# A gated mix of an S4 convolution and a top-2 SwiGLU: identity matrices by GpSimd, one sum of products on TensorE, the last tile pair in two banks, a new order

## The chip, the cores and the metric

The kernel runs on one core of a Trainium2 chip. The time is device microseconds of one execution, as a median of several runs; a profile is taken of one more execution. TensorE (PE) multiplies matrices and writes to PSUM banks; VectorE (DVE), ScalarE (ACT) and GpSimd (POOL) work elementwise; SyncE (SP) and ScalarE issue the DMA transfers of this kernel. Each engine works through its own queue of instructions, and semaphores order them between engines.

## The reference, cut to what matters

```python
x = A_u                                            # 1 x 2048 x 512, bfloat16
g = sigmoid((x * gate_w).sum(-1, keepdims=True))
a = A_ref(x, A_re, A_im, B_re, B_im, C_re, C_im, log_dt, Dskip)
b = B_ref(x, w_r, w_gate, w_up, w_down)
return g * a + (1 - g) * b

# A_ref: S4 convolution, D = 512 channels, N = 128 states, L = 2048
dt = exp(log_dt)[:, None]
P  = exp((dt * A)[:, :, None] * l[None, None, :])  # A, B, C complex
K  = einsum("dn,dnl,dn->dl", C, P, dt * B).real
y  = irfft(rfft(u, 4096) * rfft(K, 4096))[:L] + u * Dskip

# B_ref: the 2 tokens of largest x @ w_r go through silu(x_s @ w_gate) * (x_s @ w_up) @ w_down,
# times sigmoid(r), and are added to x
```

## The kernel before, in words

The convolution is done in the frequency domain with matrix products. Channels are split in two halves h of 256 (HC), tokens in two blocks `blk` of 1024, frequencies in two halves `qd`. The program is a list of some 640 operations, made by these functions in the order of L1133 to L1159:

- *Start* (L558 to L640). Six parameter tables are loaded (PRM 0 to 5: A_re, A_im, C_re, C_im, B_re, B_im), with log_dt and the identity matrix CB, a 64 KB transfer from the constant `c_bf` on SyncE's queue. DTP is exp(log_dt) on ScalarE (L586). DG (L587) is the identity with its columns scaled by DTP, a product on VectorE; RV (L588) is the identity with its columns reversed, a copy on VectorE. PE scales and transposes the parameters with DG (L597) and with the identity (L608); VectorE reduces the phase of A_im to a turn (L625 to L627, seen in the profile as L460, L459, L462) and multiplies B by C (L632, L633).
- `exps1`, `exps2`, `tab1`, `tab2` build tables of powers of exp(dt A). `turns` (L687) adds quarter turns with the identity or its negative (L709), ScalarE takes sines (L720). `trig` (L671) takes a sine, adds 16384 to its angles (L683), and takes another. `tab2` multiplies tables (L745) and joins further ones by two lists; an entry of `MUL2` with n = 1 is two products of 512 elements and a difference and a sum (L751 to L754).
- `routing` transposes u on PE (L802), copies the transposes out of PSUM (L805, four at a time 1024 wide), computes gate and router sums, and runs the two chosen tokens through the feed-forward part.
- `forward` is the transform of u (PE L945, evicted L949). `kgen` sums the kernel K in pieces (PE L964, evicted L968) and `kspec` transforms it (PE L1016, seeded by ScalarE L1009 or PE L1007, evicted L1020) into KK.
- `products(h, qds, blks)` multiplies the spectra on VectorE: p (L1039) and, for block 1, t (L1042), each 4096 wide. For block 1 the two are added (L1059), then a difference and a sum of 1024 give the real and the imaginary part (L1060, L1061), and four operations of 1024 write X (L1066). For (h, qd) = (1, 0) the additions are done by PE instead: L1052 sums p and t in PSUM with the identity and its negative, eight matmuls of 512 for each of the two parts, and L1056 evicts. This is the list `ACC`.
- `inverse(h)` is the transform back, for blocks 1 and 0 and four pairs of token tiles each. PSUM is seeded by ScalarE with u times a gate quotient (L1082), or, for the last pairs, u is scaled in place (L1080); PE adds the frequencies (L1104, eight matmuls per pair and half), and the result is scaled out: by ScalarE for most pairs (L1114), by VectorE's fused multiply-add for the pairs scaled in place (L1123), and for the last pair, tiles 5 and 7 of (h, blk) = (1, 0), in two ScalarE operations (L1126). Then it is stored, two tiles of 128 x 256 in one transfer of 128 KB (L1130).

`TT`, `TS`, `STT`, `CP`, `AC`, `EV`, `SCL` and `DMA` (L454 to L477) are the helpers that record an operation; the profile shows their lines, L455 for every `TT`, for instance. In the profile "L455 DVE TENSOR_TENSOR 128x4096" is therefore any product of that width.

The order is written out by hand. `ORDER` (L371) is a string with the list's indices in the order of work, three characters each; each engine takes its own operations in that order (L132), and `emit` (L160) puts the waits for their inputs in front. `SECOND` says for each operation that can run on two engines, (ACT, DVE) or (DVE, ACT), whether the second is taken; `PLACES` says which PSUM bank or buffer each temporary has. The new order in the change is a new `ORDER`, `SECOND` and `PLACES`.

Of the kernel before, what the change touches and what calls it, by code (L numbers as in the profile page):

```python
# [14 lines left out]
ACTF = mybir.ActivationFunctionType  # L15
ALU = mybir.AluOpType
# [236 lines left out]
ACC = ((1, 0),)  # L253
DIAG = ()
# [102 lines left out]
def small_mats():  # L357
# [15 lines left out]
    "00200r01e01h01i00000101k01m00300500400v00w00700y02000600k00f01000x01400e00800z00b01501w01602101101900900a0b101201z01301a01o01s01b00l01g02l02d01700g01u"  # L373
    "02n0b302e01r02j00h01j02301c02f02h01f02m02p02k03100d01t02g0b400q01d02r02i02o01v00j02u02q02s02t03201y01l03302v02605w02400n09k0b202w01x02a03403502503603g"
    "05v05j03h02702802909j03705k03i05x02x03803j03903k0b502204k00i00m03l00s02y03a03m05q04j00c03n04000p05p03d05e0b603o05d01805r03x03p02z03q03r00t01n03004l0b7"
    "05f06r06p03s06q06s01p03t0b804a03u04m03v0bi04n0bh04103y05l06t04o05y05t04p00u03z03w06u04q05s04204s0bj04r06v05n05m04t06x05u04u0bk04v06w04506z05z03e07006y"
    "0bm0600bl04604z0710760470750bo04304w01q07205g07707804x04c07307a07904805h0bn04906707c06804y07b05005107405i04d0bc05307d07e07o05o05407g0ba04b05204407f04e"
    "04f02c06906e04g07h02b04h05507p05606d0b905706k05806f06n0bb06m05906j0bd07j06g07m06h07r05a08v06o06l07l09l06i06207k05b07q05c0be06107n09m06307s06409n0650bf"
    "07i07t08006a07z07u09o07x09s06606b07y07v0bg08107w0c009p08209t08308408808909q06c0bp09r04i09u08609v08y08508a08c08b0bq08708x09z08i08e08d09w03b08w0br0a00a3"
    "08f0a10a208h0bs08g0by08k08l0bu09x0a60bv09y08j08m0c108n0a70a408p0bw0c20bt0a500o08r0a808u0bx08q0c90bz08o0c30a90aa09b0990ab08z08s0c509c0ac09d09e09a08t0aw"  # L380
    "0910c409f0c60c80ca09g09h0cb0cc09209i0cf0ce0da0900c70ch0ax0al0ay0az0ci0cg0cl0b00ck0960cj0970cd0co0cn0cq0cr0cm0cx0cp0cs0980ak0ct0cu0cv0cw0930cy0cz0db094"
    "03f0d10d00d30d20ev0950d40am0ao0an0d90dn0aq0df0do0ep0dc0ap0d50du0dg0ar0eq0d60dv0dw0dd0ae0dp03c0dh0as0de0di0dk0dq0dj0dl0at0dm0fd0h00dr0ds0eu0dt0d80av0fi"
    "0au0ey0f30ff0fe0eo0f40en0er0fj0d70e10fg0ex0f10fh0fk0ad0e40ew0es0af0gw0f00f70et0f20fl0ah0e50dz0ag0fm0ez0aj0e00fn0e60fo0ai0f50g60fp0gb0fq0e80ed0ea0ga0f6"
    "0f80e20g70ge0gc0eh0dy0gd0fa0gg0fr0g80fs0f90gi0e30fu0ee0ft0dx0fw0fc0e90h40ef0fb0e70eb0ei0eg0gf0g90gj0go0gh0h10ec0gk0gq0gp0gm0fv0fx0h60gx0em0el0h20fy0h7"
    "0gz0gl0gn0h30ej0h50h80ek0h90fz0g00g20hi0g10ha0g30hm0g40gy0hj0gt0g50gr0hk0hl0hn0ho0hb0hc0hp0gs0gv0gu0hs0ht0hd0he0hf0hg0hq0hh0hr"
)
SECOND = (
    "000000000000000000000000000000000000000000000100000000000000000000000000000000000000001010100000101000000000000000000000000000000000000000000000000000"
    "000000000000000000010000001000000100000000000000000000000000000000000000000000000000000000001000100000001000000000000000000000000000000000000000000000"
    "000000000000000000000000000100000000000010000000000000000000000000000000000000000000000000000000011000100000001000000000000000000000000000000000000000"  # L390
    "000000000000000000000000000000000001000000000100100000000000000000000000000000000000000000000000000000000000000000000000000000000000000000000000000000"
    "000000000010000000000000000000000000000000"
)
PLACES = (
    "023476015031122254636201420476642046744011102462062440662046000044406046674020026662010100000000014262646223660464004367063320204022041525736"
# [4 lines left out]
def bass_gated_mix__ssm_conv_s4__moe_arch_mod__prompt_kernel(nc, A_u, A_A_re, A_A_im, A_B_re, A_B_im, A_C_re, A_C_im, A_log_dt, A_Dskip,  # L400
# [24 lines left out]
    with ExitStack() as es:  # L425
# [109 lines left out]
        DD = B("dd", oR + 24 * KB, 4 * KB)  # L535
# [22 lines left out]
        DQ([(CB(0, 128, 0, (1, EK0)), cb_c[:, 0:EK0])], [], [(CB, "i")], 65536)  # L558
# [14 lines left out]
        DQ([(CB(0, 128, EK0, (1, CBW - EK0)), cb_c[:, EK0:])], [], [(CB, "o")], 196608)  # L573
# [14 lines left out]
        CP(RV(0, 128, 0, (1, 128)), CB(0, 128, 127, (-1, 128)), [CBI], [RV])  # L588
# [98 lines left out]
        def turns(h, ts):  # L687
# [23 lines left out]
            for k, g in enumerate((0, 3, 2, 1)):  # L711
# [5 lines left out]
                for x in ("cs" if k % 2 else "sc"):  # L717
                    if x == "sc"[1 - k % 2]:
                        P.op(PE, lambda hh, k=k: quarter(hh, k % 2), [TIB, CBI], [pb], cost=0.4314)
                    AC(so(2 if x == "c" else neg), lo, ACTF.Sin, [pb], [(s, x)], scale=SC16, tset=ts)  # L720
# [17 lines left out]
        def tab2(h, ts):  # L738
# [7 lines left out]
            for o, a, da, b, n in MUL2:  # L746
                A, Bc, O = lambda t: t(0, 128, a * HC, (da * HC, n), (1, HC)), lambda t: t(0, 128, b * HC, (0, n), (1, HC)), lambda t: t(0, 128, o * HC, (HC, n), (1, HC))
                p = lambda i: qa(0, 128, i * n * HC, (HC, n), (1, HC))
                kr = lambda t: [(t, k) for k in ([("e", a + i * da) for i in range(n)] + [("e", b)] if t is eb else [a + i * da for i in range(n)] + [b])]
                ko = lambda t: [(t, ("e", o + i) if t is eb else o + i) for i in range(n)]  # L750
                TT(pair(p(0), p(1)), pair(Bc(eb), Bc(di)), pair(A(eb), A(eb)), MUL, kr(eb) + kr(di), [(qa, 0), (qa, 1)])  # L751
                TT(pair(p(2), p(3)), pair(Bc(di), Bc(eb)), pair(A(di), A(di)), MUL, kr(eb) + kr(di), [(qa, 2), (qa, 3)])
                TT(O(eb), p(0), p(2), SUB, [(qa, 0), (qa, 2)], ko(eb))
                TT(O(di), p(1), p(3), ADD, [(qa, 1), (qa, 3)], ko(di))  # L754
# [40 lines left out]
        def routing():  # L795
# [42 lines left out]
            if DIAG:  # L838
                CP(SGB(0, 128, 64, (1, 16)), SG(0, 128, 96, (1, 16)), [(SG, "x")], [(SGB, "x")])
                TS(SG(0, 128, 0, (1, 16)), SGB(0, 128, 64, (1, 16)), 1.0e-30, ADD, [(SGB, "x")], [(SG, "d")])  # L840
                P.op(DVE, lambda h: h.reciprocal(SG(0, 128, 80, (1, 16)), SG(0, 128, 0, (1, 16))), [(SG, "d")], [(SG, "q")], cost=0.3)
                STT(SG(0, 128, 112, (1, 16)), SG(0, 128, 96, (1, 16)), 1.0e-30, SG(0, 128, 80, (1, 16)), ADD, MUL, [(SG, "x"), (SG, "q")], [(SG, "s")])
                TT(SG(0, 128, 112, (1, 16)), SG(0, 128, 112, (1, 16)), SG(0, 128, 64, (1, 16)), MUL, [(SG, "m")], [(SG, "s")])
# [77 lines left out]
        def late():  # L921
            P.op(POOL, lambda h: h.memset(OHR(0, 128, 0, (1, len(ERT) * 128)), 0.0), [], [OHR], cost=0.4)
            for k in (2, 3, 0, 1) if DIAG else ():
                def dd(h, k=k, act=False):
                    r = None
                    for tb in range(4 * k, 4 * k + 4):
                        o, i, c = DD(0, 128, tb * 128, (1, 128)), CB(0, 128, 0, (1, 128)), SG(0, 128, tb, (1, 1))
                        r = h.activation(out=o, in_=i, func=ACTF.Copy, scale=c) if act else h.tensor_scalar(out=o, in0=i, scalar1=c, scalar2=None, op0=MUL)
                    return r
                P.op((ACT, DVE), (lambda h, dd=dd: dd(h, act=True), dd), [CBI, (SG, "d")], [(DD, k)], cost=(1.05, 0.6))  # L930
# [65 lines left out]
        def kspec(h):  # L996
            for qd in range(2):
                for i in range(2):
                    uses = [u for u, (bi, jg) in enumerate(KUSE) if bi == i]
                    for part in range(2):  # L1000
# [3 lines left out]
                        if i:  # L1004
# [5 lines left out]
                            P.op((ACT, PE), (seed, carry), [ck, CBI], [pb], cost=(0.185 + 1024 * 0.833e-3, 0.4314))  # L1010
# [12 lines left out]
        def products(h, qds, blks):  # L1023
# [13 lines left out]
            for blk in blks:  # L1037
# [6 lines left out]
                if blk == 1 and (h, qds[0]) in ACC:  # L1044
                    for part in range(2):
                        pb = psum(2, full=True)
                        for i, b in enumerate((p, t)):
# [7 lines left out]
                            P.op(PE, acc, [CBI] + qk(b, *((0, 3), (1, 2))[part]), [pb], cost=4 * 0.2157)  # L1055
                        EV(u(part), pb(0, 128, 0, (1, 1024)), [pb], qk(p, part))  # L1056
                else:
# [10 lines left out]
        def inverse(h):  # L1068
            for blk in (1, 0):
                bufs = {}  # L1070
                tbs = lambda t2, par: [blk * 8 + (2 * t2 + e) * 2 + par for e in range(2)]
                for t2 in range(2):
                    for par in range(2):
                        pe = h in DIAG
                        mix = premix(h, blk, t2, par)
                        ts = tbs(t2, par)
                        pb = bufs[t2, par] = psum(full=True, seed=not (pe or mix))
                        for tb in ts if mix else ():
                            o = U(0, 128, tb * D + h * HC, (1, HC))
                            SCL(o, o, SG(0, 128, tb, (1, 1)), [(SG, "o")], uh(tb, h))  # L1080
                        for e, tb in enumerate(() if pe or mix else ts):
                            AC(pb(0, 128, e * 256, (1, 256)), U(0, 128, tb * D + h * HC, (1, HC)), ACTF.Copy, [(SG, "x")] + uh(tb, h), [(pb, e)], scale=SG(0, 128, 96 + tb, (1, 1)))  # L1082
                        def base(hh, pb=pb, ts=ts, pe=pe, mix=mix):
                            r = None
                            for e, tb in enumerate(ts if pe else ()):
# [122 lines left out]
```

## Time and profile before

| | us |
|---|---|
| median of 3 runs (lowest, highest) | 148.2 (148.11, 148.43) |
| the profiled execution's own time | 148.23 |
| its span in the profile | 146.4 |
| PE busy | 135.5 |
| VectorE busy | 137.7 |
| ScalarE busy | 126.1 |
| GpSimd busy | 2.3 |

The span runs from the first to the last event of the profile, and the time is 1.83 us longer. Busy times count an engine's instructions, not its waits or DMA issues. In a row of a group, "busy, mean ns" stand behind the count, and then the idle time just before, with what ended it. In a row of the timeline the first two numbers are start and length, in us from the start of the span; several instructions of one line that follow each other are one row. In the chain of work a row has start, length and what it was.

### The profile page before, as it was taken

What the parts mean: (1) busy time and instruction counts of PE and PEld (TensorE: products, weight loads), DVE (VectorE), ACT (ScalarE), POOL (GpSimd) and SP (SyncE); (2) the same over time, 40 slices, a digit from 0 to 9 for tenths busy, and PEclk for the clock granted to TensorE, in tenths of its full rate; (3) what the DMA queues carried; (4) which work ended last, traced back from release to release, by engine and by line L of the source; (5) the groups of instructions that cost most, each with busy time, mean ns of one, the idle gap of its engine ahead of it and who ended that gap; (6) DMA issues with size and microseconds to landing.
All of it is one profiled execution on the core that took longest, in us unless ns stands there. A gap on an engine that the chain in (4) does not pass through costs nothing.

```text
span 146.4 us, 3881 instructions
## 1 busy us (share of the span) xinstructions
PE 135.5 (93%) x1646; PEld 99.5 (68%) x1661; DVE 137.7 (94%) x193; ACT 126.1 (86%) x202; POOL 2.3 (2%) x10
## 2 busy tenths in 40 slices
PE   7889999799899999999879999989979999999990
PEld 2667764444656445678857899968846688888870
DVE  0699999899999999999999999999999999999982
ACT  4699999999999999999999979867997899866520
POOL 2002000000000000000000001000000000000000
PEclk9999999999999999999999999999999999999999
DMA  4999945953960004039200003879200012122224
GB/s 123 284 332 395 373 165 166 388 234 53 454 291 4 0 0 144 4 84 403 115 4 0 0 4 94 335 238 400 95 0 0 0 31 71 51 72 72 78 72 143
DMA packets 13690, 21.13 MB, mean 144 GB/s; under 512 B 2099, under 2 KB 9288, under 8 KB 13512
## 3 DMA queue, kind: packets, MB, share of 16 engines
q1 hardware_dynamic: 12696, 20.22, 39.3%
q10 hardware_dynamic: 976, 0.66, 1.5%
q8 instruction: 13, 0.21, 0.5%
q14 instruction: 5, 0.04, 0.1%
HBM read 18.78 MB, written 4.20 MB: 157 GB/s over the span
## 4 chain that ended last, share of the span: by engine, by line
PE 67%; ACT 14%; DVE 13%; issue 2%; DMA 2%; SPq 0%; DVEq 0%
PE ps L1104 18%; PE ps L945 15%; PE ps L1016 10%; ACT AR L470 8%; PE ps L964 7%; DVE AR L455 6%; DVE AR L462 3%; ACT AR L474 3%; PE ps L1052 2%; ACT AR L466 2%; DVE AR L470 2%; PE ps L976 2%; DMA AR<-c_bf 2%; PE ps L709 1%; DVE AR L620 1%
## 5 line engine op out<-in xcount | busy, mean ns | idle before, releaser
L455 DVE TENSOR_TENSOR AR<-AR 128x1024 bf16<-128x1024 bf16 (+7 forms) x133 | 115.3, 926 | 3.1 <-DMA AR<-c_bf 2.7
L470 ACT ACTIVATE AR<-ps 128x1024 bf16<-128x1024 f32 (+7 forms) x65 | 51.8, 840 | 4.6 <-PE ps L1016 1.7
L466 ACT ACTIVATE AR<-ps 128x1024 bf16<-128x1024 int16 (+2 forms) x34 | 28.7, 907 | 1.9 <-PE ps L597 1.8
L945 PE MATMUL ps<-AR 128*128 128x512 bf16 x120 | 28.8, 379 | 0.9 <-ACT AR L470 0.5
L1104 PE MATMUL ps<-AR 128*128 128x256 bf16 x256 | 29.3, 273 | 0.1
L1104 PEld LDWEIGHTS ps<-AR 128*128 128x128 bf16 x256 | 24.9, 98 | 3.7 <-ACT ps L466 0.3
L945 PEld LDWEIGHTS ps<-AR 128*128 128x128 bf16 x128 | 11.9, 97 | 13.9 <-ACT AR L470 1.1
L964 PEld LDWEIGHTS ps<-AR 128*128 128x128 bf16 x512 | 18.5, 97 | 1.5
L964 PE MATMUL ps<-AR 128*128 128x84 bf16 (+1 forms) x512 | 18.8, 196 | 0.0
L1016 PE MATMUL ps<-AR 128*128 128x256 bf16 x160 | 18.8, 273 | 0.0
L1016 PEld LDWEIGHTS ps<-AR 128*128 128x128 bf16 x160 | 15.3, 98 | 3.3 <-ACT AR L470 0.5
L474 ACT ACTIVATE AR<-AR 128x256 int32<-128x256 f32 (+3 forms) x27 | 15.4, 597 | 0.1
L1114 ACT ACTIVATE AR<-ps,AR 128x256 bf16<-128x256 f32 x24 | 9.9, 474 | 3.9 <-PE ps L1104 3.6
L466 ACT ACTIVATE ps<-AR 128x256 f32<-128x256 bf16 x26 | 11.3, 483 | 0.0
L466 ACT ACTIVATE AR<-AR 128x1024 bf16<-128x1024 int16 (+4 forms) x12 | 9.3, 788 | 0.0
L645 PE MATMUL ps<-AR 128*128 128x464 bf16 x22 | 6.8, 440 | 0.9 <-DVE AR L648 0.9
L455 DVE TENSOR_TENSOR AR<-AR,ps 128x2048 bf16<-128x2048 bf16 (+1 forms) x6 | 7.2, 1213 | 0.0
L704 PE MATMUL ps<-AR 128*128 128x512 f16 x24 | 6.2, 379 | 0.0
L709 PE MATMUL ps<-AR 128*128 128x512 bf16 x13 | 4.1, 382 | 1.4 <-ACT AR L466 1.3
L802 PE MATMUL ps<-AR 128*128 128x128 bf16 x64 | 4.6, 219 | 0.1
L1052 PE MATMUL ps<-AR 128*128 128x512 bf16 x15 | 3.6, 379 | 1.2 <-ACT AR L474 1.2
L462 DVE SCALAR_TENSOR_TENSOR AR<-ps,AR 128x256 bf16<-128x256 f32 (+2 forms) x8 | 4.1, 538 | 0.5 <-PE ps L1104 0.3
(70 smaller groups left out, 87.8 us busy)
## 6 DMA issues: line engine op xcount, KB each, us to landing
AR<-c_ksp SPq DMA_DIRECT2D x5, 512.0 KB, 4.8
AR<-in_A_u_dram SPq DMA_DIRECT2D x8, 256.0 KB, 5.1
AR<-out_dram SPq DMA_DIRECT2D x4, 512.0 KB, 5.5
AR<-c_inv SPq DMA_DIRECT2D x1, 2048.0 KB, 8.9
AR<-in_B_w_gate_dram SPq DMA_DIRECT2D x1, 1792.0 KB, 8.7
AR<-in_B_w_up_dram SPq DMA_DIRECT2D x1, 1792.0 KB, 9.6
out_dram<-AR SPq DMA_DIRECT2D x14, 128.0 KB, 2.2
AR<-c_fwd SPq DMA_DIRECT2D x4, 256.0 KB, 5.2
```

The source lines that it names most:

```text
L455: return P.op(DVE, lambda h: h.tensor_tensor(out=o, in0=a, in1=b, op=op), rd, wr, cost=tt_cost(o, a, b), **k)
L462: return P.op(DVE, lambda h: h.scalar_tensor_tensor(out=o, in0=a, scalar=sc, in1=b, op0=op0, op1=op1), rd, wr, cost=0.16 + nel(o) * 1.02e- ...
L466: return P.op(ACT, lambda h: h.activation(out=o, in_=a, func=func, scale=scale, bias=bias), rd, wr, cost=0.185 + nel(o) * 0.833e-3 + (0.09 ...
L470: return P.op((ACT, DVE), (lambda h: h.activation(out=o, in_=a, func=ACTF.Copy), lambda h: h.tensor_copy(o, a)), rd, wr, cost=(0.185 + n * ...
L474: return P.op((ACT, DVE), (lambda h: h.activation(out=o, in_=a, func=ACTF.Copy, scale=c), lambda h: h.tensor_scalar(out=o, in0=a, scalar1= ...
L645: r = h.matmul(pb(0, 128, 0, (1, 464)), MSB(0, 128, 0, (0, 128)), MSB(0, 128, 0, (0, 464)), start=True, stop=True)
L945: last = h.matmul(pb(0, 128, j * 512, (1, 512)), F[ft](0, 128, (kt * 2 + 1 - j) * 128, (1, 128)), pm[q](0, 128, kt * 512, (1, 512)), start ...
L964: last = hh.matmul(pb(0, 128, g // k * 512 + g % k * W4 + o, (1, n)), TP[h][1 - i // 2](0, 128, (b0 + g) * 128, (1, 128)), r[i](0, 128, (b ...
L1016: last = hh.matmul(pb(0, 128, n * 256, (1, 256)), KP[u](0, 128, tau * 128, (1, 128)), KC[h](0, 128, jg * 256, (1, 256)), start=(k == 0 and ...
L1052: r = hh.matmul(pb(0, 128, pm * 512, (1, W)), CB(0, 128, 128 * (k if part == 0 else 0), (1, 128)), b(0, 128, ((0, 3), (1, 2))[part][k] * 2 ...
L1104: r = hh.matmul(pb(0, 128, e * 256, (1, 256)), G(0, 128, ((par * 2 + part) * 4 + ft) * 512 + (2 * t2 + e) * 128, (1, 128)), X(0, 128, h * ...
L1114: return [hh.activation(out=U(0, 128, tb * D + h * HC, (1, HC)), in_=pb(0, 128, tb // 2 % 2 * 256, (1, HC)), func=ACTF.Copy, scale=SG(0, 1 ...
```

## The change

1. *Identity matrices.* CB's first 128 columns and RV are no longer loaded and copied: for each, GpSimd sets 128 x 128 to zero and runs `affine_select`, which writes 1.0 on the diagonal (the anti-diagonal for RV). The 64 KB load on SyncE and VectorE's copy go. The negative identity, the second 128 columns, comes with the later transfer of the remaining constants, and the PE steps that use it (L709, L1007, L1052) depend on that.
2. *ACC.* For (h, qd) = (1, 1) the real part's sum of p and t goes to PE (eight matmuls and one eviction); VectorE adds only the middle 2048 of the 4096, and the imaginary part as before.
3. *MUL2 with n = 1.* One product of 1024 in place of two of 512. There is one such entry for each channel half. The rows of the temporaries for n = 2 change places, with the same operations.
4. *The last pair.* Tiles 5 and 7 of (1, 0) have a PSUM bank each, half used, so that their PE steps are separate operations. Stores of (1, 0) are eight of 64 KB, four each from SyncE and ScalarE, in place of four of 128 KB.
5. *Removed:* the parts of the code for the empty list `DIAG`.
6. *Order.* In the start, SyncE issues log_dt, A_im, C_re, B_re and then u; ScalarE issues C_im, A_re and B_im, all ahead of the Exp (before, B_im was issued after it). On GpSimd the two identity pairs come first. On PE the four matmuls for A_im come ahead of A_re's eight. Later, the products (0) of block 0 come behind those of block 1 of both halves, tile 7's steps of the inverse come ahead of the other pairs' last ones and tile 5's at the very end.
7. *Engines* by `SECOND`. To VectorE: one eviction of the routing transposes (1024), two tiny operations (of 16 elements or so), one scaling to int32 of 256, one "+16384" on 1024 int32 (L683), one scaling of u in place (256), and tile 5's last scaling. To ScalarE: one scaling of 1024 in `turns` (bfloat16).

```diff
-ACC = ((1, 0),)
-DIAG = ()
+ACC = {(1, 0): (0, 1), (1, 1): (0,)}
...
-        DQ([(CB(0, 128, 0, (1, EK0)), cb_c[:, 0:EK0])], [], [(CB, "i")], 65536)
+        def diag(b, key, sign, base):
+            P.op(POOL, lambda h: h.memset(b, 0.0), [], [key], cost=0.5)
+            P.op(POOL, lambda h: h.affine_select(out=b, in_=b, compare_op=ALU.not_equal, fill=1.0, base=base, pattern=[[sign, 128]], channel_multiplier=1), [], [key], cost=1.0)
+        diag(CB(0, 128, 0, (1, 128)), (CB, "i"), -1, 0)
+        diag(RV(0, 128, 0, (1, 128)), RV, 1, -127)
...
-        DQ([(CB(0, 128, EK0, (1, CBW - EK0)), cb_c[:, EK0:])], [], [(CB, "o")], 196608)
+        DQ([(CB(0, 128, 128, (1, CBW - 128)), cb_c[:, 128:])], [], [(CB, "o")], 196608)
...
-        CP(RV(0, 128, 0, (1, 128)), CB(0, 128, 127, (-1, 128)), [CBI], [RV])
...
+                if n == 1:
+                    w1 = lambda t, k: t(0, 128, k * HC, (1, HC))
+                    Q = lambda x, y, z, w: pair(pair(x, y), pair(z, w))
+                    TT(Q(*[p(i) for i in range(4)]), Q(*[w1(t, b) for t in (eb, di, eb, di)]), Q(*[w1(t, a) for t in (eb, eb, di, di)]), MUL, kr(eb) + kr(di), [(qa, i) for i in range(4)])
...
-                    for part in range(2):
+                    for part in ACC[h, qds[0]]:
...
+                    if len(ACC[h, qds[0]]) == 1:
+                        v = lambda b: b(0, 128, 2 * W, (1, 4 * W))
+                        TT(v(p), v(p), v(t), ADD, qk(t, 1, 2), qk(p, 1, 2))
+                        TT(u(1), u(1), u(2), ADD, qk(p, 2), qk(p, 1))
...
-                tbs = lambda t2, par: [blk * 8 + (2 * t2 + e) * 2 + par for e in range(2)]
+                units = [(t2, par, es) for t2 in range(2) for par in range(2) for es in (((0,), (1,)) if (h, blk, t2, par) == (1, 0, 1, 1) else ((0, 1),))]
...
-                    DMA([(dr(out, token(blk, st, 0, 0) * D + h * HC, (2 * D, 128), (D, 2), (1, HC)), U(0, 128, tb * D + h * HC, (D, 2), (1, HC)))],
-                        uh(tb, h) + uh(tb + 1, h), [], 131072, tag="final", eng=ACT if (h, blk) == (1, 0) and st % 2 else SP)
+                    for pars in ((0,), (1,)) if (h, blk) == (1, 0) else ((0, 1),):
+                        t0, k = tb + pars[0], len(pars)
+                        DMA([(dr(out, token(blk, st, pars[0], 0) * D + h * HC, (2 * D, 128), (D, k), (1, HC)), U(0, 128, t0 * D + h * HC, (D, k), (1, HC)))],
+                            [x for t in range(t0, t0 + k) for x in uh(t, h)], [], 65536 * k, tag="final", eng=ACT if (h, blk) == (1, 0) and (st + pars[0]) % 2 else SP)
```

More of the change, by code (lines that the diff above doesn't have):

```diff
@@ L377 @@
[L377 to L380, printed above, removed]
@@ L1070, in inverse @@
                 bufs = {}
-                tbs = lambda t2, par: [blk * 8 + (2 * t2 + e) * 2 + par for e in range(2)]
-                for t2 in range(2):
-                    for par in range(2):
-                        pe = h in DIAG
-                        mix = premix(h, blk, t2, par)
[L1076 to L1085, printed above, removed]
-                                r = hh.matmul(pb(0, 128, e * 256, (1, 256)), DD(0, 128, tb * 128, (1, 128)), U(0, 128, tb * D + h * HC, (1, HC)), start=(e == 0), stop=False, skip_group_check=True)
-                            for e, tb in enumerate(ts):
-                                if tb in ERT:
-                                    r = hh.matmul(pb(0, 128, e * 256, (1, 256)), OHR(0, 128, ERT.index(tb) * 128, (1, 128)), ZB(0, 128, h * HC, (1, HC)), start=mix and r is None, stop=False, skip_group_check=True)
-                            return r
-                        ne = sum(tb in ERT for tb in ts)
-                        if pe or ne:
-                            P.op(PE, base, ([(DD, tb // 4) for tb in ts] + [x for tb in ts for x in uh(tb, h)] if pe else []) + ([OHR, (ZB, "y"), (ZB, ("e", h)), (ZB, "d")] if ne else []), [pb], cost=(2 * pe + ne) * 0.1092)
```

149 lines of the change are left out of this document (78 added, 71 removed).

## The prediction, made before the changed kernel ran

> **What bounds the kernel now.** I read the page first, then VectorE's waits, the table of windows, the end of the chain, and last the start of the timeline.
>
> ```profile
> span 146.4 us, 3881 instructions
> PE 135.5 (93%) x1646; PEld 99.5 (68%) x1661; DVE 137.7 (94%) x193; ACT 126.1 (86%) x202; POOL 2.3 (2%) x10
> ```
>
> Two engines are nearly full, VectorE (DVE) at 137.7 and TensorE (PE) at 135.5 of 146.4 us. So the question is which of them ever lets the other wait. VectorE's waits (total, times, longest):
>
> ```profile
> DVE AR L455 <- DMA AR<-c_bf: 2.7, 1, 2.7
> DVE AR L460 <- PE ps L597: 1.0, 1, 1.0
> ...
> DVE AR L847 <- PE ps L851: 0.4, 1, 0.4
> DVE AR L462 <- PE ps L1104: 0.3, 1, 0.3
> ```
>
> Two waits of 2.7 and 1.0 us stand at the start, one of 0.4 in the routing, one of 0.3 in the tail. Nothing else in the program holds VectorE up. The windows say the same (length, then busy time and count of PE, PEld, DVE, ACT, POOL, then granted clock, DMA share, GB/s):
>
> ```profile
> 10.00:140.55 130.55, 125.35 (x1568) 92.79 (x1581) 129.60 (x178) 118.66 (x190) 1.33 (x4) 1.00 0.39 140
> 110.10:140.84 30.74, 30.65 (x265) 25.73 (x265) 30.24 (x31) 22.81 (x54) 0.00 (x0) 1.00 0.18 53
> ```
>
> From 10 to 140.55 us VectorE is busy 129.60 of 130.55. PE has 5.2 us of slack there, but in the last 30.74 us it has 30.65 busy: it runs behind VectorE's products with nothing to spare. The tail (chain, timeline, DMA rows):
>
> ```profile
> 137.33 3.51 PE ps L1104 x32
> ...
> 140.87 2.82 DVE L462 SCALAR_TENSOR_TENSOR AR<-ps,AR 128x256 bf16<-128x256 f32 x6 [0.32 <-PE ps L1104]
> out_dram<-AR ACTq DMA_DIRECT2D x2, 128.0 KB, 2.2
> ```
>
> PE ends at 140.84, VectorE's six closing operations (0.47 each) end at 143.69, and the last store takes the rest, 2.7 us with its issue. So the bound is VectorE's total work plus what it waits at the start. The profiled execution took 148.23 us, 1.83 more than its span; the median shown is 148.2. I sum against 148.23.
>
> **The change part by part.**
>
> *Start.* Rows of the timeline (start, length), the chain and the DMA rows:
>
> ```profile
> 0.74 0.52 POOL L577 MEMSET AR<- 128x512 bf16 x1 [0.29 <-POOLq L1193]
> 1.20 0.42 SPq L477 DMA_DIRECT2D AR<-c_bf  x1
> 1.67 1.28 ACT L466 ACT_TABLE_LOAD   x1 [1.67 <-PEq L1193]
> 2.94 0.33 ACTq L477 DMA_DIRECT2D AR<-in_A_B_im_dram  x1
> 2.97 0.20 ACT L466 ACTIVATE AR<-AR 128x4 bf16<-128x4 bf16 x1
> 3.55 0.69 DVE L455 TENSOR_TENSOR AR<-AR 128x512 bf16<-128x512 bf16 x1 [2.68 <-DMA AR<-c_bf]
> 4.30 1.92 PE L597 MATMUL ps<-AR 128*128 128x128 bf16 x16 [0.18 <-DVE AR L455]
> 4.30 1.06 PE ps L597 x8
> 5.39 0.69 DVE L460 TENSOR_SCALAR AR<-ps 128x512 f32<-128x512 f32 x1 [1.04 <-PE ps L597]
> 7.65 0.40 PE L597 MATMUL ps<-AR 128*128 128x128 bf16 x4 [0.75 <-DMA AR<-in_A_B_im_dram]
> AR<-c_bf SPq DMA_DIRECT2D x1, 64.0 KB, 2.3
> AR<-in_A_B_im_dram ACTq DMA_DIRECT2D x1, 128.0 KB, 4.7
> ```
>
> DG, the first product (L455), needs the identity and dt (the Exp on ScalarE). The identity landed at 1.20 + 2.3 = 3.5; dt was ready at 2.97 + 0.20 = 3.17. After the change the load of B_im is issued ahead of the Exp, one issue slot of about 0.45 earlier in ScalarE's queue, so table load and Exp come 0.45 later: dt at 3.62, DG at about 3.65, 0.10 late. The identity is then GpSimd's: memset, select, memset, select. Its memset rows:
>
> ```profile
> L653 POOL MEMSET AR<- 128x256 bf16 x2 | 0.6, 312 | 0.0
> L1193 POOL MEMSET const-bfloat16-1.0<- 128x1 bf16 x1 | 0.1, 101 | 0.0
> ```
>
> A 128-wide memset lies between 0.10 and 0.31, say 0.21. From 0.74 the identity is in time for 3.6 if a select takes under (3.6 − 0.74 − 0.42)/2 = 1.2 us. No row shows a select. Its bounds by these rows are 0.10 and 0.53 (the 512-wide memset), and I take 0.31: ready at 1.8, hidden. Its cover fails above 1.2 us, and then each us counts twice, once for each select.
>
> The Trainium skill ("GPSIMD Engine Reference", section 2.1, Instruction dispatch) speaks against this: the first call to a freshly loaded GpSimd kernel pays about 6 µs for loading its code, unseen in a profile. No row here shows such a gap behind GpSimd's first operations; by that page alone, as an estimate, the identity would come near 7.8 and the kernel would take about 152 us.
>
> What gains is the order on PE. Before, eight matmuls (A_re's) stood between DG and the sums that L460 reads, 1.06 us for the eight with four of them for L460 itself; after, the four of A_im come first, 0.53. So L460 starts at 5.39 + 0.10 − 0.53 = 4.96, a gain of **0.43**. The next wait is for the last four matmuls (B_im, 7.65): B_im, issued at about 1.66, lands at 6.4 by the 4.7 row, and PE's 28 matmuls in a row end by about 7.4, ahead of the product that needs them (8.08 − 0.43 = 7.65). Bounds: −0.43 and, if some of it is lost at that point, −0.1. The dropped copy RV fell into VectorE's 1.04 wait and is worth nothing. The −identity now comes in a later, larger transfer; its first reader on PE (a quarter of a turn, L709) comes after 27 us, and I cost that at nothing.
>
> *VectorE's work.* Rows grouped by form (busy, mean ns), and a stretch of the timeline:
>
> ```profile
> L455 DVE TENSOR_TENSOR AR<-AR 128x4096 bf16<-128x4096 bf16 x15 | 34.0, 2286 | 0.1
> L455 DVE TENSOR_TENSOR AR<-AR 128x2048 bf16<-128x2048 bf16 x22 | 26.6, 1210 | 0.0
> L455 DVE TENSOR_TENSOR AR<-AR 128x1024 bf16<-128x1024 bf16 x40 | 25.9, 683 | 0.2
> L455 DVE TENSOR_TENSOR AR<-AR 128x512 bf16<-128x512 bf16 x21 | 8.5, 421 | 2.7 <-DMA AR<-c_bf 2.7
> L470 DVE COPY AR<-ps 128x1024 bf16<-128x1024 bf16 x6 | 3.9, 682 | 0.0
> L474 DVE TENSOR_SCALAR AR<-AR 128x1024 bf16<-128x1024 bf16 x3 | 1.2, 406 | 0.0
> L474 DVE TENSOR_SCALAR AR<-AR 128x256 int32<-128x256 f32 x3 | 0.9, 285 | 0.0
> L459 DVE TENSOR_SCALAR AR<-AR 128x512 f32<-128x512 f32 x1 | 0.4, 427 | 0.0
> L459 DVE TENSOR_SCALAR AR<-AR 128x16 bf16<-128x16 f32 x2 | 0.4, 223 | 0.0
> 101.92 8.50 DVE L455 TENSOR_TENSOR AR<-AR 128x4096 bf16<-128x4096 bf16 x6
> ```
>
> The last row holds three of 4096 and three of 1024: 3 × 2.286 + 3 × 0.683 = 8.91 by means, 8.50 by the clock, so neighbours overlap by about 0.07. I use start-to-start times: 2.22, 1.14, 0.61, 0.35.
>
> - *Removed:* the 4096-wide sum and the 1024-wide difference of the last product (2.22 + 0.61), four 512-wide table products (1.40), one 1024-wide scaling moved to ScalarE (0.34): 4.57.
> - *Added:* a 2048-wide sum (1.14), two 1024-wide table products (1.22), one eviction of the routing transposes (0.61), two tiny operations (0.30), one scaling to int32 and one premix of 256 (0.20 each), tile 5's last scaling at 0.47 (as the closing operations), and the "+16384" on 1024 int32.
>
> The last has no row. Below it lies the bf16 row, 0.34; above it the 512-wide read from PSUM at 0.69 (L460, in the start's rows), doubled and less the overlap, 1.3. The nearest is the 512-wide f32 in SBUF at 0.43: two fixed parts less, 0.64, which I take. Added: 4.78; net **+0.21**, from −0.09 to +0.87.
>
> The one 1024-wide table product is thus not worth a fixed cost of four: it drops two of four, 1.40 − 1.22 = 0.18. The sum moved to TensorE is worth 2.83 − 1.14 = 1.69, and the operations moved over from ScalarE spend it.
>
> *TensorE and ScalarE.* Rows of the chain, of a group and of the timeline:
>
> ```profile
> 112.66 2.59 PE ps L1052 x12
> L470 ACT ACTIVATE AR<-ps 128x1024 bf16<-128x1024 f32 x34 | 34.2, 1027 | 2.3 <-PE ps L1016 1.7 <-PE ps L1052 0.6
> 112.70 0.84 ACT L1114 ACTIVATE AR<-ps,AR 128x256 bf16<-128x256 f32 x2 [0.98 <-PE ps L1104]
> 113.42 1.27 ACT L466 ACTIVATE ps<-AR 128x256 f32<-128x256 bf16 x3
> ```
>
> The added sum is eight matmuls of 512, 0.216 each: 1.73 us of PE, and one eviction of 1.03 on ScalarE. ScalarE's total still falls by about 2 us. The new wait is VectorE's: its X writes (L1066) for half 1 read that eviction. From T0, the end of the second product of half 1, PE has in the new order the sixteen older matmuls' second half, nine steps of the inverse (eight matmuls each, 0.87 by the row of 32 in 3.51), one of kspec and the eight new ones: some 12.1 us, the eviction ends at 13.2. ScalarE has 5 long operations, 3 pairs of finals, 10 seeds and a tiny one after T0 + 1.8: 13.0 in a row, 14.6 by single rows. VectorE has three of 4096, one of 2048 and eleven of 1024 first: 14.5. So the wait is covered by −0.1 to +1.3, and I take 0.6. Cost: nothing. At the end PE's extra 1.73 us may stay hidden: before, PE ended 2.85 ahead of VectorE, and in the new order its last step has only one operation of VectorE behind it.
>
> *Tail.* The last bank is now tile 5's alone and its scaling (VectorE) is the last thing, with the 0.47 counted above. It can start when PE ends; from VectorE's last X write PE has nine steps of 2 or 4 matmuls, 28 × 0.11 = 3.1 us, VectorE its six closing operations and one premix, 3.0. The wait of 0.32 ahead of those shrinks, by about half, **−0.15** (−0.3 to 0). The last store is 64 KB in place of 128: the 64 and 128 KB rows have 2.3 and 2.2, so I give it **−0.1** (−0.1 to +0.1).
>
> *Sum:* −0.43 + 0.21 − 0.15 − 0.1 = −0.47, so 148.23 − 0.47 = **147.8 us**, 0.4 below the median shown.
>
> **The rivals.**
>
> 1. *Nothing comes of it.* The gain at the start is lost at B_im's matmuls (−0.1), or the int32 operation runs at the PSUM rate (+0.66): −0.47 + 0.33 = −0.14 or −0.47 + 0.66 = +0.19, about 148.2. Against it: the 512-wide f32 row.
> 2. *TensorE's extra sum becomes a wait (slower).* The place is the X write behind the new eviction. If one more step of inverse(0) (0.87) and one more eviction (1.03) stand ahead of it than my count has, it is 1.9 late against a cover of 0.6: +1.3, and the kernel ends at 149.1. It decides from a lateness of 0.6 + 0.5. For it: PE's 30.65 of 30.74. Against it: ScalarE loses 2 us of work.
> 3. *The identity comes late (slower).* A select of 2.5 us is 2.6 late: 147.8 + 2.6 = 150.4. It decides from a select of 1.2 us. For it: no row shows a select. Against it: GpSimd's rows are all of 0.10 to 0.53 us.
>
> **How the numbers follow.** Forecast (147.1 to 148.1) 0.52; nothing comes of it 0.16; TensorE's wait 0.20; identity late 0.12. About 0.2%, 0.3 us, is what can be told from no change: faster is under 147.9, slower over 148.5. Faster: 0.45 of the forecast's 0.52. Same: the other 0.07 and rival 1, 0.23. Slower: rivals 2 and 3, 0.32. The range: at the low end the start's −0.43, the routing's wait of 0.4 gone in the new order, −0.09 of work and −0.25 of tail, 147.1, less 0.1 for the spread of the runs shown; at the high end rival 2's 149.1 and the same 0.1, 149.2. Rival 3 is left out, with a little of rival 2.
>
> **What would show it.** Right: DG still at 3.6 to 3.7, L460 at about 5.0; selects under 0.6 us; VectorE's total within 137.5 to 138.5; no wait of VectorE over 0.3 after 30 us; TensorE up by 1.7 and ScalarE down by 2. Wrong: a VectorE wait on PE or ScalarE in the last 40 us (rival 2), DG later than 4 (rival 3), an int32 row above 1 us (rival 1). The forecast also fails if the new order leaves VectorE waiting somewhere before 100 us, where I checked no step.

## The result, and the profile after

The changed kernel takes 147.81 us (median of 7 runs, 147.26 to 148.09) beside 148.55 for the kernel before on the same chip (148.11 to 149.29): a ratio of 0.9935, 95% interval 0.9905 to 0.9964, or 0.5 to 1.4 us less. In a later comparison of the same two the ratio was 0.9942 (0.9924 to 0.9960). The forecast was 147.8 against 148.2, a gain of 0.47; the measured medians are 0.74 apart. Ratios leave out runs over 1.5% above the fastest of their kernel, medians don't, which matters most for f2 below.

The profiled execution took 148.09 us, hardly less than the one of before (148.23). The page and VectorE's waits of the changed kernel (total, times, longest):

```profile
span 146.3 us, 3922 instructions
PE 138.1 (94%) x1669; PEld 101.9 (70%) x1669; DVE 137.3 (94%) x195; ACT 125.0 (85%) x197; POOL 3.2 (2%) x14
```

```profile
DVE AR L455 <- ACT AR L466: 2.8, 1, 2.8
DVE AR L460 <- PE ps L599: 1.1, 1, 1.1
...
DVE AR L455 <- PE ps L957: 0.5, 1, 0.5
DVE AR L470 <- PE ps L809: 0.3, 1, 0.3
DVE AR L848 <- PE ps L852: 0.3, 1, 0.3
DVE AR L455 <- PE ps L599: 0.2, 1, 0.2
```

ScalarE is down by 1.1 us, VectorE by 0.4. TensorE reads 2.6 more, but this can't be set against the 1.7 that was forecast: the page of before counts 1646 matmuls beside 1661 weight loads, this one 1669 of each, so fifteen matmuls are missing from the earlier record (f3, the kernel before in another order, has 1661). For the same reason the 5.2 us of slack that the prediction read for TensorE (x1568 beside x1581) is too much. Of VectorE's waits the first two are about as long as before and the wait of 0.3 in the tail is gone. Three are new: 0.2 at the products with C (8.4 us), 0.3 in the routing (16.4 us) and, the longest, 0.5 at kgen's matmuls (L957, 66.7 us). The windows that were shown of before, now:

```profile
10.00:140.55 130.55, 126.87 (x1592) 94.02 (x1593) 128.87 (x179) 119.39 (x189) 1.09 (x3) 1.00 0.38 136
110.10:140.84 30.74, 30.51 (x264) 25.45 (x263) 30.57 (x36) 25.43 (x59) 0.00 (x0) 1.00 0.14 40
```

VectorE is busy 128.87 of 130.55, where it was 129.60. The end and the start of the timeline:

```profile
143.57 0.48 DVE L1118 TENSOR_SCALAR AR<-ps,AR 128x256 bf16<-128x256 f32 x1
out_dram<-AR ACTq DMA_DIRECT2D x4, 64.0 KB, 1.7
```

```profile
1.17 0.29 POOL L559 TENSOR_SCALAR_AFFINE_SELECT AR<-AR 128x128 bf16<-128x128 bf16 x1 [0.23 <-POOL AR L558]
...
1.76 0.29 POOL L559 TENSOR_SCALAR_AFFINE_SELECT AR<-AR 128x128 bf16<-128x128 bf16 x1
...
2.15 1.28 ACT L466 ACT_TABLE_LOAD   x1 [2.15 <-issue]
...
3.45 0.21 ACT L466 ACTIVATE AR<-AR 128x4 bf16<-128x4 bf16 x1
3.69 0.69 DVE L455 TENSOR_TENSOR AR<-AR 128x512 bf16<-128x512 bf16 x1 [2.82 <-ACT AR L466]
...
4.44 1.89 PE L599 MATMUL ps<-AR 128*128 128x128 bf16 x8 [0.23 <-DVE AR L455]
...
5.51 0.69 DVE L460 TENSOR_SCALAR AR<-ps 128x512 f32<-128x512 f32 x1 [1.13 <-PE ps L599]
...
8.38 2.35 DVE L455 TENSOR_TENSOR AR<-AR,ps 128x1024 f32<-128x1024 bf16 x2 [0.20 <-PE ps L599]
```

Set this against the span of before. The products with C start at 8.38, 0.30 later than before. From there to VectorE's last end it is 135.67 us (8.38 to 144.05), before 135.61: 0.06 more, as the terms 0.21 and −0.15 said. Behind VectorE's last end the span (146.27 to two digits, before 146.45) has 2.22 us left, before 2.76: 0.54 less, where 0.1 was said. So in this execution the start lost over half of what the last store won. L460 begins at 5.51 though only four matmuls stand ahead of it: eight took 1.89 us, and before, sixteen took 1.92. Their starts are 0.213 us apart, in the profile before 0.109.

### The profile page after: what moved, and what is told of

It reads as the page before. It is cut to its first block, busy times and chain, and to the rows that moved or that the text cites. A ratio compares the mean times of both kernels' runs of the same rounds, so it can differ in the third digit from the quotient of the medians.

```text
span 146.3 us, 3922 instructions
## 1 busy us (share of the span) xinstructions
PE 138.1 (94%) x1669; PEld 101.9 (70%) x1669; DVE 137.3 (94%) x195; ACT 125.0 (85%) x197; POOL 3.2 (2%) x14
## 4 chain that ended last, share of the span: by engine, by line
PE 49%; DVE 44%; ACT 2%; issue 2%; ACTq 1%; DVEq 0%
DVE AR L455 39%; PE ps L1098 17%; PE ps L938 14%; PE ps L957 3%; PE ps L1045 2%; PE ps L599 2%; DVE AR L462 2%; PE ps L647 1%; DVE AR L622 1%; PE ps L700 1%; PE ps L825 1%; PE ps L905 1%; PE ps L795 1%; ACTq L477 1%; PE ps L711 1%
## 5 line engine op out<-in xcount | busy, mean ns | idle before, releaser
L455 DVE TENSOR_TENSOR AR<-AR 128x1024 bf16<-128x1024 bf16 (+6 forms) x130 | 113.5, 933 | 3.6 <-ACT AR L466 2.8
L470 ACT ACTIVATE AR<-ps 128x1024 bf16<-128x1024 f32 (+7 forms) x63 | 51.1, 851 | 5.5 <-PE ps L1009 3.0
L938 PE MATMUL ps<-AR 128*128 128x512 bf16 x128 | 30.0, 379 | 0.0
L1098 PEld LDWEIGHTS ps<-AR 128*128 128x128 bf16 x256 | 24.9, 98 | 3.3
L938 PEld LDWEIGHTS ps<-AR 128*128 128x128 bf16 x128 | 12.1, 98 | 12.9
L957 PEld LDWEIGHTS ps<-AR 128*128 128x128 bf16 x512 | 18.1, 96 | 0.9
L957 PE MATMUL ps<-AR 128*128 128x84 bf16 (+1 forms) x512 | 18.4, 196 | 0.0
L1009 PEld LDWEIGHTS ps<-AR 128*128 128x128 bf16 x160 | 15.5, 98 | 3.1
L1045 PE MATMUL ps<-AR 128*128 128x512 bf16 x24 | 5.8, 379 | 0.2 <-DVE AR L455 0.2
L647 PEld LDWEIGHTS ps<-AR 128*128 128x128 bf16 x22 | 2.2, 113 | 4.2 <-issue 1.4
L809 PEld LDWEIGHTS ps<-AR 128*128 128x128 bf16 x64 | 3.7, 98 | 1.9 <-DVE AR L455 1.5
```

The lines of the kernel that those rows point to most:

```text
L455: return P.op(DVE, lambda h: h.tensor_tensor(out=o, in0=a, in1=b, op=op), rd, wr, cost=tt_cost(o, a, b), **k)
L470: return P.op((ACT, DVE), (lambda h: h.activation(out=o, in_=a, func=ACTF.Copy), lambda h: h.tensor_copy(o, a)), rd, wr, cost=(0.185 + n * ...
L647: r = h.matmul(pb(0, 128, 0, (1, 464)), MSB(0, 128, 0, (0, 128)), MSB(0, 128, 0, (0, 464)), start=True, stop=True)
L809: last = h.transpose(bb(0, 128, db * 256 + t_ * 128, (1, 128)), U(0, 128, (2 * q + t_) * D + db * 128, (1, 128)), RV(0, 128, 0, (1, 128)) ...
L938: last = h.matmul(pb(0, 128, j * 512, (1, 512)), F[ft](0, 128, (kt * 2 + 1 - j) * 128, (1, 128)), pm[q](0, 128, kt * 512, (1, 512)), start ...
L957: last = hh.matmul(pb(0, 128, g // k * 512 + g % k * W4 + o, (1, n)), TP[h][1 - i // 2](0, 128, (b0 + g) * 128, (1, 128)), r[i](0, 128, (b ...
```

## The experiments

Lines of order are shown with what the operations do. Every time is beside the kernel before on the same chip (148.55 to 148.67). Kernels in which a line of code was dropped have line numbers one lower.

**a0. The changed kernel once more.**

> The changed kernel once more, for its spread and a second look at its start. Theory: the moment at which TensorE's matmuls go from 0.107 to 0.056 us (128 columns) differs from execution to execution, whatever the kernel; in the first profile of the changed kernel it came at 6.5 us, in that of the kernel before at 3.9. In this profile it may lie anywhere between 3.9 and 7; if it lies before 4.4, VectorE's L460 starts near 5.05 and the span is about 145.7. Rival: the changed kernel's start itself (a gap of 0.24 us instead of 0.18 before the first matmul on DG) delays it; then it is at 6.5 again in this profile and in every variant of the changed kernel. Median 147.4 to 147.9 either way.

147.86 us (6 runs), ratio 0.9942 (0.9924 to 0.9960). Its matmuls on DG were 0.213 apart again; they became fast at 6.2 us. This alone can't tell the two apart; the profiles of the others do. In e2, e5, f2 and the last one, whose starts are the changed kernel's, they were 0.109 apart from the first on. e5's profile:

```profile
4.43 1.05 PE L599 MATMUL ps<-AR 128*128 128x128 bf16 x8 [0.28 <-DVE AR L455]
5.08 0.69 DVE L460 TENSOR_SCALAR AR<-ps 128x512 f32<-128x512 f32 x1 [0.70 <-PE ps L599]
```

Same instructions, same start, 1.05 us instead of 1.89, and L460 at 5.08. Over the fourteen profiles the pace doubles anywhere between 3.9 and 6.8 us. The twelve of them that recorded a granted clock begin this record at that moment, wherever matmuls run to show it: at 3.91 us in the kernel before and at 6.58 in the changed one. The rival (the kernel's own start delays it) falls. The Trainium skill ("TensorE: Matmul & The Clock Gate", Part 1: The HAM clock gate) has a rule for it: the clock is halved until an activity window of about 3.4 µs was busy, and that window runs free of the kernel, so the moment varies from run to run. The trace agrees that the moment varies; its spread of 2.9 us is wider than the ±500 ns that the same part of the Trainium skill states.

**e1. A_re's first four matmuls ahead again.**

```diff
 TensorE, behind the warm-up:
-A_im x4 (L460 reads it), A_re x4, transposes of C x8, ...
+A_re x4, A_im x4 (L460 reads it), transposes of C x8, ...
```

> Undoes one step of the new order on TensorE: A_re's first four matmuls go ahead of A_im's four again. Theory that VectorE's work bounds everything behind its first wait: it starts L460 later by four matmuls, 0.43 us where a matmul of this form takes 0.109 and 0.85 where it takes 0.213, so the median is 0.4 to 0.85 us above the changed kernel's, 148.2 to 148.6. Rival: the load of B_im or a later wait sets VectorE's start anyway, and nothing changes (within 0.2 us).

148.01 us, ratio 0.9969 (0.9951 to 0.9986): 0.15 us over the changed kernel by medians, 0.4 by ratios. Its profile had the slow pace:

```profile
6.36 0.69 DVE L460 TENSOR_SCALAR AR<-ps 128x512 f32<-128x512 f32 x1 [1.99 <-PE ps L599]
```

L460 starts 0.86 later than in a0 (5.50), as expected for four slow matmuls. VectorE ends only 0.55 later (144.44 against 143.89). Of the 0.31 between, 0.18 is the wait at kgen, which shrank from 0.50 to 0.32. The order pays, and part of it is taken back at kgen. (A_re has twelve matmuls in all; only its first four stood ahead of A_im's before.)

**e2. Last stores of 128 KB.**

```diff
-for pars in ((0,), (1,)) if (h, blk) == (1, 0) else ((0, 1),):
+for pars in ((0, 1),):
```

> Undoes the splitting of the last stores: four of 128 KB, the last one for tiles 4 and 5. Theory from the two profiles: the last store took 2.14 us from issue to the last wait with 128 KB and 1.61 with 64 KB, so this costs 0.5 us over the changed kernel, 148.3. Rival, the prediction's own term: 0.1 us, 147.9.

148.20 us, ratio 0.9994 (0.9956 to 1.0031): 0.34 more by medians, 0.8 by ratios with a wide interval. In its profile the last store ends 2.23 us after its issue, in a0's 1.61, and the span ends 2.78 behind VectorE, in a0's 2.23. By the profiles the store is worth some 0.5, and the rival (0.1) falls.

**e3. The sum of products of (1, 1) back on VectorE.**

```diff
-ACC = {(1, 0): (0, 1), (1, 1): (0,)}
+ACC = {(1, 0): (0, 1)}
```

> Undoes the sum of products on TensorE for the second frequency half of channel half 1: VectorE adds 4096 and subtracts 1024 again, TensorE has 1.73 us less and ScalarE an eviction less. Theory: VectorE's total is the bound, so the time rises by 2.22 + 0.61 - 1.14 = 1.69 us, to about 149.5. Rival: TensorE, full from 100 us on in the changed kernel's profile, is the bound by now; then the time stays or falls by up to 1.7 us.

150.21 us, ratio 1.0101 (1.0076 to 1.0126): 2.35 over the changed kernel.

```profile
139.72 6.61 SPq L476 DMA_DIRECT2D out_dram<-AR  x9
...
145.20 0.48 DVE L1117 TENSOR_SCALAR AR<-ps,AR 128x256 bf16<-128x256 f32 x1
```

VectorE ends at 145.67, 1.78 after a0's 143.89, for the 1.69 expected. The rest, 0.5, lies behind VectorE's end. There SyncE's row of nine closing stores (6.61 us, waits for data included) ends at 146.33, 0.66 behind VectorE, where a0's ends at 143.86, just ahead of it; how much of the 0.5 this makes was not tried. VectorE's work is the bound, and TensorE is not.

**e4. The "+16384" back on ScalarE** (`SECOND` of that operation; 1.07 us there).

> The one operation of 1024 int32 (add 16384) goes back from VectorE to ScalarE, where it takes 1.07 us. Theory: VectorE's total is the bound, so the time falls by 0.6 us (0.683 in the trace, less the overlap of 0.07), to about 147.2. Rival: ScalarE, full in this stretch, then hands its sine tables over later, VectorE waits for them, and the time stays or rises by up to 1.1 us.

148.41 us, ratio 0.9969 (0.9947 to 0.9992): 0.55 slower than the changed kernel, though VectorE has 0.6 less to do. Two of its waits:

```profile
DVE AR L474 <- ACT AR L466: 0.8, 1, 0.8
...
DVE AR L848 <- PE ps L852: 0.7, 1, 0.7
```

The rival is right in its result, and in part in its cause. The first wait, for ScalarE, is new. The second was 0.11 and is for TensorE: in a0 the "+16384" runs on VectorE (23.93 to 24.61) between two steps of the routing and fills the time until TensorE's result is there. Together the two waits grew by 1.44 us in the stretch from 24 to 27 us. By this trace the 0.6 us of work that VectorE saves would have gone into the second wait even with ScalarE in time.

**e5. The wait at 66.6 us filled.**

```diff
 VectorE:
-weights of half 1 (1024, waits for kgen of half 0), table product (1.22 us), ...
+table product (1.22 us), weights of half 1 (1024), ...
```

> Takes away the wait of 0.50 us that the new order has at 66.6 us, where VectorE is to write the weights of half 1 (L773 of the changed kernel) over rows that TensorE's kgen (L957) still reads: the table product of 1.22 us behind it goes ahead of it. Theory that such a wait costs the whole its length: 0.5 us less than the changed kernel, 147.3. Rival: TensorE and ScalarE run behind by as much at the next place, and the wait comes back there: no change (within 0.2 us).

147.09 us (146.90 to 147.58), ratio 0.9892 (0.9861 to 0.9922): 0.77 below the changed kernel, and the wait at L957 doesn't come back at another place. From the start of L460 to VectorE's end it is 0.54 less than in a0 (137.85 against 138.39), the length of the wait. What makes the rest of the 0.77 was not shown; TensorE's pace at the start, which differs by run, moves L460 by up to 0.43. VectorE's waits behind the start:

```profile
DVE AR L470 <- PE ps L809: 0.3, 1, 0.3
DVE AR L848 <- PE ps L852: 0.3, 1, 0.3
```

**e6. Identity by DMA, its mirror by a copy.**

```diff
-diag(CB(0, 128, 0, (1, 128)), (CB, "i"), -1, 0)
-diag(RV(0, 128, 0, (1, 128)), RV, 1, -127)
+DQ([(CB(0, 128, 0, (1, EK0)), cb_c[:, 0:EK0])], [], [(CB, "i")], 65536)
...
+CP(RV(0, 128, 0, (1, 128)), CB(0, 128, 127, (-1, 128)), [CBI], [RV])
```

> The identity comes by DMA again (64 KB, second on SyncE's queue) and its mirror by VectorE's copy; all else as in the changed kernel. Theory: both lie in the cover of the Exp, which is ready at 3.66 in the changed kernel (a landing near 3.5, a copy of 0.19 in VectorE's wait for TensorE), so nothing changes, 147.7 to 148.0. Rival: the issue slot of 0.46 us and 64 KB ahead of A_im, C_re and B_re make those late, and the time rises by up to 0.5 us.

148.22 us, ratio 0.9975 (0.9949 to 1.0001): 0.36 over the changed kernel by medians, 0.5 by ratios.

```profile
5.24 1.03 PE L598 MATMUL ps<-AR 128*128 128x128 bf16 x8 [1.04 <-DMA AR<-in_A_A_im_dram]
5.88 0.69 DVE L459 TENSOR_SCALAR AR<-ps 128x512 f32<-128x512 f32 x1 [1.40 <-PE ps L598]
```

The Exp starts when it does in the changed kernel (3.44), so the identity is covered, but TensorE now waits for A_im: it was issued a slot later and took 3.5 us to land, where it took 2.4 to 2.6 in the changed kernel. L460 (here L459) starts at 5.88, with the fast pace, against 5.08. The rival is right. That a load of 64 KB stands ahead of A_im's does not alone make it slow: it stands there in the kernel before and in f3 too, and A_im took 2.6 and 2.9. There B_im's load is issued at 2.9 rather than 1.66; whether that is the difference was not tried.

**e7. The Exp 0.48 us earlier.**

```diff
-prm_l(0, eng=ACT)
+prm_l(0)   # issued behind B_re
 TensorE:
-A_im x4, A_re x4, transposes of C x8, A_re x8, B x8
+A_im x4, transposes of C x8, B x8, A_re x4, A_re x8
```

> A_re is loaded by SyncE behind B_re in place of ScalarE, so that ScalarE's table load and Exp come 0.48 us earlier; on TensorE the transposes of C and the scaling of B go ahead of A_re's twelve matmuls. Theory: DG then starts at 3.22 instead of 3.69, L460 0.47 earlier, and the time falls by 0.3 to 0.5 us, to about 147.4, as the start is on VectorE's path. Rival: ScalarE gets A_re's sums about 0.8 us later and is full for the next 60 us, so VectorE waits for its tables: no gain, or up to 0.8 us slower.

148.60 us, ratio 0.9982 (0.9959 to 1.0005): 0.74 slower than the changed kernel. VectorE's waits:

```profile
DVE AR L455 <- ACT AR L466: 2.3, 1, 2.3
DVE AR L470 <- PE ps L809: 1.1, 2, 0.7
```

The first is 0.5 shorter, as wanted. Evictions of the routing transposes then wait 0.73 and 0.13 more for TensorE; the 0.35 is there in a0 too. The rival is right in its size and its cause, though VectorE waits at another place than it said. In the trace ScalarE starts on A_re's sums at 6.83 (a0: 6.34), works from there without a gap, and makes an eviction of these transposes at 13.58 (a0: 13.09); TensorE's next transposes wait 0.65 for it, and VectorE waits for those.

**f1. The last pair in one bank.**

```diff
-units = [... for es in (((0,), (1,)) if (h, blk, t2, par) == (1, 0, 1, 1) else ((0, 1),))]
+units = [... for es in ((0, 1),)]
```

> Undoes the two banks of the last pair: tiles 5 and 7 share a bank again, TensorE's steps for both come at the very end (16 matmuls in place of 8 behind the other pairs), and tile 7's scaling on ScalarE and its store move to the end, beside tile 5's on VectorE. TensorE's total is the same. Theory: the end is set by TensorE's last matmul, then VectorE's operation of 0.48 and one store, which tile 7's now only accompany, so the time is that of the changed kernel or up to 0.2 us more. Rival: the early steps of tile 7 are what keeps TensorE fed while VectorE writes its last X, and without them TensorE ends up to 0.9 us later.

148.24 us, ratio 0.9967 (0.9951 to 0.9984): 0.38 over the changed kernel, more than the 0.2 of the theory; the rival, TensorE later by up to 0.9, is right in kind.

```profile
143.55 0.48 DVE L1117 TENSOR_SCALAR AR<-ps,AR 128x256 bf16<-128x256 f32 x1 [0.29 <-PE ps L1097]
144.06 0.47 ACT L1117 ACTIVATE AR<-ps,AR 128x256 bf16<-128x256 f32 x1 [6.16 <-DVE AR L1117]
```

TensorE ends 0.29 us behind VectorE's other work, and ScalarE's scaling of tile 7 does not run beside VectorE's of tile 5: it waits for it, as they read the same bank and the program orders them. In the profile the first makes the way from L460 to VectorE's end 0.28 longer than in a0, and behind that end the span has 2.59 left for a0's 2.23. Two banks take both away.

**f2. Two more waits filled,** by operations of 1.1 and 1.2 us that stood behind them.

```diff
 VectorE, beside e5's swap:
-eviction of transposes (waits 0.35), ..., table product (1.1 us)
+table product (1.1 us), eviction of transposes, ...
-second maximum's index (waits 0.28), ..., table product (1.2 us)
+table product (1.2 us), second maximum's index, ...
```

> The changed kernel with three waits of VectorE filled: the one at 66.6 us as before, and the next two (0.35 us at 16.2 before an eviction of the routing transposes, 0.28 at 30.8 before the second index), each by an operation of 1.1 to 1.2 us that stood behind it. Theory that each wait of VectorE costs its length: 0.5 + 0.35 + 0.28, to about 146.7, and 0.4 to 0.6 below the kernel with the first alone. Rival: TensorE, which reads that eviction and that index and is full from 100 us on, gets them up to 1.1 us later, and nothing is won over 147.1.

149.45 us by the median of 12 runs (148.07 to 151.71), ratio 1.0007 (0.9971 to 1.0044): all that e5 had won is lost. Half of the runs lie from 148.07 to 148.88, and these, like the profile (148.09), are some 1.1 over e5.

```profile
16.29 1.09 DVE L455 TENSOR_TENSOR AR<-AR 128x1792 bf16<-128x1792 bf16 x1 [0.95 <-ACT AR L466]
...
19.82 0.19 DVE L470 CAST AR<-ps 128x32 bf16<-128x32 f32 x1 [0.72 <-PE ps L825]
```

The operation put into the gap of 0.35 waits 0.95 itself, for ScalarE, and 0.72 follows at the routing, whose transposes came later.

**f3. The kernel before, with A_im's four matmuls first.**

```diff
 TensorE (kernel before):
-A_re x4, A_im x4, A_re x8, ...
+A_im x4, A_re x4, A_re x8, ...
```

> The kernel before with one part of the change alone: on TensorE A_im's four matmuls go ahead of A_re's first four. Theory: it gains nothing there, as the products that need B_im (at 8.08) still wait for its load (landing at 7.65, matmuls until 8.05), 148.4 to 148.7; only with B_im issued ahead of the Exp does the earlier L460 count. Rival, the prediction's term taken by itself: 0.43 us faster, 148.1.

150.47 us by the median (148.98 to 150.93), ratio 1.0093 (1.0061 to 1.0126): slower by 1.4 us by the ratio, which neither theory had. Its runs fall into two groups, four of 148.98 to 149.20 and eight of 149.85 to 150.93, so the loss may be as little as 0.4.

```profile
4.65 2.91 PE L597 MATMUL ps<-AR 128*128 128x128 bf16 x16 [0.44 <-DMA AR<-in_A_A_im_dram]
5.70 0.69 DVE L460 TENSOR_SCALAR AR<-ps 128x512 f32<-128x512 f32 x1 [1.25 <-PE ps L597]
8.04 0.69 DVE L470 COPY AR<-ps 128x1024 bf16<-128x1024 bf16 x1 [0.47 <-PE ps L608]
```

With the 64 KB of the identity ahead of it in SyncE's queue, A_im lands after DG is ready, so the matmuls that were to go first hold up all the others. In this profile (149.85), at the slow pace until 6.7 us, L460 is 0.31 late, the copy waits 0.47 more, and two waits in the routing grow by 0.8. How much of that is the pace and how much the order stays open.

**f4. Two waits filled,** e5's and the second of f2.

> The changed kernel with two waits of VectorE filled, those at 66.6 us (0.50) and 30.8 us (0.28); the one at 16.2 us is left as it is, since the operation put ahead of it had to wait 0.95 us for ScalarE itself. Theory: 0.5 + 0.28 below the changed kernel, about 147.0, and 0.1 to 0.3 below the kernel with the first swap alone. Rival: the index of the second token comes 1.2 us later to its gather and products, and that costs the 0.28 again: as the first swap alone, 147.1 to 147.4.

147.06 us (146.76 to 147.70), ratio 0.9908 (0.9883 to 0.9932). Both waits are gone from its profile; beside e5 (147.09) no difference is to be seen. e5 and f4 beat both kernels.

## Why the prediction held, step by step

That 147.8 was met so closely is in part luck. The sum started from 148.23, while the kernel before runs at 148.55 by the median, and the gain is 0.74 rather than 0.47. Errors cancel in it: the unforeseen wait of 0.50 against closer starts of VectorE's operations and the tail's wait, and the start, which gained less than was booked, against the last store, which gained some 0.4 more. By its own signs the prediction is right for DG (3.69), the selects (0.29), the int32 row (0.68) and VectorE's waits at the end. It missed L460 in that profile (5.51 for about 5.0), VectorE's total (137.3, just under its 137.5), ScalarE's fall (1.1 for 2) and the wait over 0.3 after 30 us, which it had named as a way to fail.

- *VectorE's work is the bound:* right, by e3 (1.78 at VectorE's end for 1.69). The rival with TensorE's wait at the new eviction didn't come: VectorE shows no wait behind 100 us. There was less room than the prediction thought. It read TensorE's end in the kernel before as 140.84, 2.85 ahead of VectorE's, but that is where the chain passes to VectorE. The matmuls run on to 142.57, 1.12 ahead, and in the changed kernel to 143.46, 0.58 ahead (before, then after):

```profile
137.17 5.40 PE L1104 MATMUL ps<-AR 128*128 128x256 bf16 x48
136.28 7.18 PE L1098 MATMUL ps<-AR 128*128 128x256 bf16 x64
```

- *The start, −0.43:* the mechanism is right, the size depends on TensorE's pace, which the prediction took from one execution. L460 is at 5.08 with the fast pace (forecast 4.96; DG came at 3.69, not 3.65) and at 5.51 with the slow one, before 5.39 with the fast one. At equal pace the gain is thus 0.31. The four matmuls cost 0.86 in e1, at the slow pace.
- *The identity hidden, its transfer booked at nothing:* the second half of this step failed. The selects took 0.29 (0.31 taken) and were ready at 2.05, and the Exp covers either source, as said. What the prediction missed is the slot that the transfer leaves in SyncE's queue. A_im takes it; without that L460 starts at 5.88 (e6) or 5.70 (f3), later than the 5.39 of the kernel before. Rival 3 is refuted, and so is the time that the 6 µs of the Trainium skill's "GPSIMD Engine Reference", section 2.1, would give here: no select pays it.
- *Work +0.21 and tail wait −0.15:* the sum was right (+0.06 from 8.38 to the end), the parts were not. The tail's wait of 0.32 went whole. Gaps of over 0.06 us between the first products with C and VectorE's end grew from 0.80 to 1.31, so the rest shrank by some 0.46 where +0.21 was added. In the trace 13 instead of 17 operations, besides those behind these gaps, start only after the end of the one before them (0.03 us behind it) rather than some 0.08 ahead of it. That would make 0.45 of the 0.67 between; it was counted, not tried.
- *The int32 operation at 0.64:* it took 0.683, less the overlap 0.61. But the sum booked it as a loss, and e4 shows that on ScalarE it costs 0.55 more: on VectorE it fills a wait of 0.6 for TensorE, and it takes away one of 0.8 for ScalarE.

```profile
L685 DVE TENSOR_SCALAR AR<-AR 128x1024 int32<-128x1024 int32 x1 | 0.7, 683 | 0.0
```

- *The last store, −0.1:* mis-sized; it measured −0.54 to −0.6. The row of 128 KB that it was taken from (2.2) is of stores and fits the last one (2.13 from issue to landing). The row of 64 KB (2.3) is of a load at the start; the last store of 64 KB takes 1.59. Of the 0.54 between them, 0.20 is the issue itself, 0.34 us for 64 KB against 0.54.
- *The last pair in two banks:* the forecast booked 0.47 for tile 5's scaling and no gain; against one bank the split is worth 0.38 (f1).
- *Not foreseen:* the wait of 0.50 at kgen, which the new order brought. The prediction said that it had checked no step before 100 us. Undone, it gives another 0.77 by the medians, of which the profiles show 0.54 (e5).

## What to carry to other kernels

Where one engine is full, its own total forecasts the time well, but terms of half a microsecond hang on what the others hand it: look for each new wait of that engine, in the order of its queue, before summing its work. A transfer that is off the path still holds a slot ahead of the next one, so ask what moves up when it goes. Fill a wait with an operation only after checking that this one's inputs are ready.

## What the runs showed of the hardware that was not expected

- TensorE's pace at the start doubles at a moment that differs by execution, from 3.9 to 6.8 us over fourteen profiles, while the granted clock of the windows reads 1.00 throughout: the clock's record begins only at that moment (6.58 in the changed kernel), and the windows from 0 to 5 and from 5 to 10 us show 1.00 all the same. So read the pace from the spacing of equal matmuls. It moves L460 by 0.43 us from one start to another that is the same (5.08 in e5 and 5.51).
- At the fast pace the matmuls of 128 columns on DG whose output is spread over the bank (wide form, L599) start 0.109 apart. The matmuls on DG whose output is contiguous (B's eight, also L599) and the transposes (L610) start 0.056 apart.
- The last store of 64 KB ends 1.61 us after its issue, that of 128 KB 2.14 to 2.23.
